# Mixer after pooled attention, one core: alpha1 spread by a DMA, the first batch's order of work changed

## The chip, the cores and the metric

The kernel runs on one core of one Trainium2 chip. The metric is the device time of one execution in microseconds; before the change it is 352.65 us, the median of three runs (352.64, 352.65 and 353.04). The profile is that of one further execution and covers a span of 351.1 us.

## The reference

Two blocks follow each other, for 8 batches of 576 tokens. Attention has 8 heads of 64; keys and values are averaged over groups of 8 tokens, so that each of the 576 queries meets 72 keys. Its output x, 576 x 512 for each batch, goes into a mixer:

```
k_p = k.reshape(B, H, Sp, 8, D).mean(axis=3)            # v_p alike
attn = softmax(q @ k_p.T / sqrt(D));  x = attn @ v_p
a1  = alpha1 * x + beta1
tok = einsum('ts,bsd->btd', w_tok, a1)
u   = x + lam * tok
ch  = relu((alpha2 * u + beta2) @ w_ch1) @ w_ch2
out = u + lam * ch
```

alpha1, beta1, alpha2, beta2 and lam are vectors over the 512 columns; w_tok is 576 x 576, w_ch1 512 x 2048, w_ch2 2048 x 512. Inputs and output are float32 in memory; matrices are multiplied in 16-bit types.

## The kernel before, in words

**Tiling.** A batch is cut into four chunks of 128 tokens and a rest of 64; two batches share one chunk for their rests. Nine blocks of four chunks go through the hidden layer. For a block, `mlp_A` (L604) makes one of 16 hidden slices of 128 x 512 and `mlp_B` (L638) turns all 16 into the output of one chunk.

**Order of work.** Each engine takes its instructions strictly in the order in which the program emits them, and waits where an operand or a buffer isn't ready. For blocks in the steady state the order comes from a list of due times that is sorted (at the end of the function). The attention and mix of batch 1 are worked into block 0 in this way, those of batch 2 into block 1, and so on. Batch 0 has nothing to be worked into: its order is written out by hand, call after call, ahead of the loop. Nearly all of the change is in this written order.

**Batch 0.** `att_F` transposes two heads' queries on TensorE and copies them to `qT`; heads 0 to 3 come from the first half of q, 4 to 7 from the second. `cast_rem` makes the 16-bit remainder rows (tokens 512 to 575) and `att_Frem` transposes its queries. `double_k` and `att_K` make the averaged keys; `first_V` the averaged values. `att_S` makes one head's scores (L455, L458) and exponentials on ScalarE (L460), `att_AV` its output (L519, L523), which VectorE divides by the row sum (L525, L527) into the tile `x`.

**The mix.** The operand of the token mix is `xs` = lam * alpha1 * x in 16 bits, made by `att_X` two heads at a time: L534 for the four full chunks, L538 for the rest of 64 rows. The product lam * alpha1, spread over 128 partitions, is `lamal_bc`. The term with beta1 is a row more of `xs` (`bias_row`, L258), which meets the row sums of w_tok. `setup_wtok(c)` transposes one column block of w_tok into `wtT` (copy on ScalarE, L299), and `setup_rowsum(c)` puts that block's row sums into a spare row of `wtT` (L308, L310). `mix_T(b, c)` multiplies one chunk (L567, five matmuls of 128 x 512; the fifth reads the rest rows of `xs`), adds x on VectorE to give u (L571), and multiplies by alpha2 into `u_bf` (L574, on VectorE or GpSimd). `mix_uT` transposes `u_bf` (L588) and copies it to `u_fm` (L590), the operand of `mlp_A`. `setup_bias` makes the hidden layer's bias from beta2 and w_ch1 (L349).

**How vectors are spread.** lam, alpha1 and beta1 come as rows into `vecs`. `broadcast` spreads a row by a matmul with a column of ones (L278) and copies it out of PSUM; for alpha1 VectorE multiplies by lam while it copies (L282). alpha2 is spread by a DMA instead (`load_al2`, L273), behind a memset of one column of its tile, so that the transfer can't start before a chosen point of VectorE's order.

**Queues.** SP and ScalarE issue some loads, GpSimd issues those that cast to 16 bits (q, w_tok, w_ch1, w_ch2, the first k and v). During the first 50 us GpSimd's queue always holds work. The later loads of SP are held by memsets on VectorE: al2, then the remainder rows of batch 1 (L119), then its k (L90).

**Buffers.** PSUM tiles named gp (`gp(...)`) take turns in six banks, two more serve the outputs of the hidden layer and the warm-up matmuls (`keep_warm`, L558: matmuls of 128 x 512 whose result nobody reads).

Of the kernel before, what the change touches and what calls it, by code (L numbers as in the profile page):

```python
# [7 lines left out]
FP = mybir.dt.float32  # L8
# [3 lines left out]
ALU = mybir.AluOpType  # L12
AX = mybir.AxisListType

P = 128
SPG = 72
DM = 512
# [6 lines left out]
def kernel(  # L24
# [18 lines left out]
    nc = tc.nc  # L43
    ctx.enter_context(tc.manual_schedule())
    B, H, S, D = q.shape
# [19 lines left out]
    st1 = {}  # L65
# [75 lines left out]
    def cast_rem(b, eng, copy=None):  # L141
        raw = st1[b]["rem_raw"]
        rq = work.tile([P, 2, 2, D], BF, tag="rem_q", bufs=2, name="rem_q")
        rk = work.tile([P, 2, 2 if b else 3, D], BF, tag="rem_k", bufs=2, name="rem_k")
        (copy or eng.tensor_copy)(out=rq.rearrange("p c h d -> p h c d"), in_=raw[:, 0])  # L145
        twice = [raw[:, 1, :, c].unsqueeze(2).to_broadcast((P, 2, 2, D)) for c in range(2)]
        if b:
            eng.tensor_tensor(out=rk, in0=twice[0], in1=twice[1], op=ALU.add)
        st1[b]["rem"] = rq, rk
# [27 lines left out]
    al2_bc = const.tile([P, DM], FP, tag="al2_bc", name="al2_bc")  # L177
    b2row = const.tile([4, P], FP, tag="b2row", name="b2row")

    vecs = const.tile([65, 4, DM], FP, tag="vecs", name="vecs")  # L180
    ones_row = const.tile([1, P], FP, tag="ones_row", name="ones_row")
    nc.vector.memset(ones_row, 1.0)

    def load_vector(i, src, queue=nc.scalar):
        n = 65 if i in (0, 3) else 1
        queue.dma_start(out=vecs[0:n:64, i],
                        in_=src.unsqueeze(0).to_broadcast((1 + n // 65, DM)))

    new_batch(0)
    load_vector(0, moe_lam)  # L190
    load_rem(0)
    load_q_bf(0, 0)
    load_k16(0, 0)
    load_vector(1, moe_alpha1, nc.sync)
    load_vector(3, moe_beta1, nc.sync)
    start = const.tile([1, 2], FP, tag="start", name="start")
    nc.vector.memset(start, 0.0)
    nc.scalar.activation(out=start[:, 1:2], in_=start[:, 0:1], func=AF.Exp, bias=0.0, scale=1.0)
# [56 lines left out]

    def bias_row(i):
        p0 = 64 - 64 * i
        nc.vector.tensor_tensor(out=xs_pool[i][p0:p0 + 1, 4, :], in0=vecs[p0:p0 + 1, 3],  # L258
                                in1=vecs[p0:p0 + 1, 0], op=ALU.mult)

    b2c_bf = const.tile([P, 4], BF, tag="b2c_bf", name="b2c_bf")
# [3 lines left out]
    def more_constants():  # L265
        nc.vector.memset(ones_bf, 1.0)
        nc.vector.memset(ones_lo[0:64], 1.0)
        nc.vector.memset(ones_lo[64:128], 0.0)
        nc.vector.memset(wtT[:, :, S:640], 0.0)

    def load_al2(behind):
        behind.memset(al2_bc[:, 0:1], 0.0)
        nc.sync.dma_start(out=al2_bc, in_=moe_alpha2.unsqueeze(0).to_broadcast((P, DM)))  # L273

    def broadcast(i, out, by=None):

        ps = gp("ps_bc")
        nc.tensor.matmul(out=ps, lhsT=ones_row, rhs=vecs[0:1, i])  # L278
        if by is None:
            nc.scalar.copy(out=out, in_=ps)  # L280
        else:
            nc.vector.tensor_tensor(out=out, in0=by, in1=ps, op=ALU.mult)  # L282

    def setup_vectors():
        ps = gp("ps_vec")
# [68 lines left out]
    def att_F(b, hp, copy=nc.scalar.copy):  # L354


        st = st1[b]
        u, r = hp // 2, hp % 2
        if r == 0:
            st["qT"][u] = work.tile([P, 8, P], BF, tag="qT", bufs=4, name="qT")  # L360
        if b > 1:
            if r == 0:
                nc.sync.dma_start_transpose(out=st["qT"][u],
                                            in_=st["q"][u].rearrange("p h c d -> p (h c d)"))
            return
        ps_q = gp("ps_q").bitcast(BF)
        for c in range(4):
            nc.tensor.transpose(
                out=ps_q[:, 128 * c:128 * c + 128],
                in_=st["q"][u][:, 2 * r + c // 2, 2 * (c % 2):2 * (c % 2) + 2].rearrange(  # L370
                    "p c d -> p (c d)"),
                identity=identity_bf)
        copy(out=st["qT"][u][:, 4 * r:4 * r + 4, :],
                       in_=ps_q[:, 0:512].rearrange("p (c t) -> p c t", c=4))
# [16 lines left out]
    def double_k(u):  # L391

        nc.vector.tensor_copy(out=st1[0]["k"][u][:, :, 4], in_=st1[0]["k"][u][:, :, 0])
        if u == 0:
            cast_rem_k(nc.vector)
# [52 lines left out]
    def att_S(b, h):  # L448
        st = st1[b]
        u, r, hh = h // 4, h // 2 % 2, h % 2  # L450
        ET = ET_pool[u][:, h % 4]
        for half in range(2):
            n0, n = 256 * half, 256 + 64 * half
            ps_sc = gp("ps_sc")
            nc.tensor.matmul(out=ps_sc[0:SPG, 0:256], lhsT=kpT_pool[u][:, half, h % 4, :],  # L455
                             rhs=st["qT"][u][:, 2 * (h % 4):2 * (h % 4) + 2, :])
            if half:
                nc.tensor.matmul(out=ps_sc[0:SPG, 256:320], lhsT=kpT_pool[u][:, hh, h % 4, :],  # L458
                                 rhs=st["rem_qT"][:, :, h // 2::4].rearrange("p c i -> p i c"))
            nc.scalar.activation(out=ET[:, n0:n0 + n], in_=ps_sc[0:SPG, 0:n],  # L460
                                 func=AF.Exp, bias=0.0, scale=0.125)
        st["ET"][h] = ET
# [45 lines left out]
    def att_AV(b, h):  # L508
        st = st1[b]
        if "x" not in st:  # L510
            st["x"] = st1[b - 1]["x"] if b % 2 else work.tile([P, 6, DM], FP, tag="x_tm", bufs=1, name="x_tm")
        hp, hh = h // 2, h % 2
        ET, vp1, x = st["ET"][h], vp1_pool[hp], st["x"]
        ps_av = gp("ps_av")
        av = ps_av[:, 0:5 * 66].rearrange("p (c x) -> p c x", x=66)
        odd = b % 2
        for c in range(4):
            m0 = 256 * (c % 2) + 128 * (c // 2)
            nc.tensor.matmul(out=av[:, odd + c, :], lhsT=ET[:, m0:m0 + 128],  # L519
                             rhs=vp1[:, hh, :])  # L520

        r0 = 512 - 64 * odd
        nc.tensor.matmul(out=av[:, 4 - 4 * odd, :], lhsT=ET[:, r0:r0 + 128], rhs=vp1[:, hh, :])  # L523
        rec = work.tile([P, 5], FP, tag="rec", bufs=2, name="rec")
        nc.vector.reciprocal(out=rec, in_=av[:, :, 64:65])  # L525
        dd = D * h
        nc.vector.tensor_tensor(out=x[:, 1 - odd:6 - odd, dd:dd + D], in0=av[:, :, 0:64],  # L527
                                in1=rec.unsqueeze(2).to_broadcast((P, 5, D)), op=ALU.mult)

    def att_X(b, h0, h1, eng=nc.vector):  # L530

        x, xs = st1[b]["x"], xs_pool[b % 2]
        cols = slice(D * h0, D * h1)
        eng.tensor_tensor(  # L534
            out=xs[:, 0:4, cols], in0=x[:, 1:5, cols],
            in1=lamal_bc[:, cols].unsqueeze(1).to_broadcast((P, 4, D * (h1 - h0))), op=ALU.mult)
        p0 = 64 * (b % 2)
        eng.tensor_tensor(out=xs[p0:p0 + 64, 4, cols], in0=x[p0:p0 + 64, 5 - 5 * (b % 2), cols],  # L538
                          in1=lamal_bc[p0:p0 + 64, cols], op=ALU.mult)


    st2 = {}
# [11 lines left out]
    def keep_warm(count):  # L554

        ps = psB.tile([P, DM], FP, tag="ch", bufs=2, name="ps_warm")
        for _ in range(count):
            nc.tensor.matmul(out=ps, lhsT=warm[:, 0:P], rhs=warm)  # L558
# [98 lines left out]
    load_q_bf(1, 0)  # L657
    load_q_bf(1, 1)
    load_w1(2)
    keep_warm(2)  # L660
    broadcast(0, lam_bc)
    keep_warm(2)
    att_F(0, 0)
    att_F(0, 1)
    more_constants()
    cast_rem(0, nc.vector)
    att_Frem(0, nc.scalar.copy)
    keep_warm(1)
    double_k(0)
# [5 lines left out]
    first_V(0, 0)  # L675
    att_S(0, 2)
    double_k(1)
    att_AV(0, 0)
    att_S(0, 3)
    keep_warm(1)  # L680
    att_K(0, 1, None)
    att_AV(0, 1)
    broadcast(1, lamal_bc, lam_bc)
    att_F(0, 2)
    att_F(0, 3, nc.vector.tensor_copy)
    att_X(0, 0, 2, nc.gpsimd)
    att_AV(0, 2)
    keep_warm(1)
    att_S(0, 4)
    first_V(0, 1)  # L690
    att_AV(0, 3)
    att_X(0, 2, 4, nc.gpsimd)
    load_al2(nc.vector)
    att_S(0, 5)
    setup_vectors()
    keep_warm(1)
    att_AV(0, 4)
    att_S(0, 6)
    keep_warm(1)
    att_AV(0, 5)  # L700
    load_rem(1, behind=nc.vector)
    att_X(0, 4, 6, nc.gpsimd)
    att_S(0, 7)
    setup_wtok(0, nc.scalar.copy)
    att_AV(0, 6)
    setup_wtok(1, nc.scalar.copy)
    att_AV(0, 7)
    for u in range(2):
        load_k(1, u, nc.vector)
    setup_rowsum(0)  # L710
    setup_wtok(2, nc.scalar.copy)
    setup_rowsum(1)
    setup_wtok(3, nc.scalar.copy)
    att_X(0, 6, 8)
    setup_rowsum(2)
    keep_warm(1)
    load_w1(3)
    load_v16(1, (0, 1))
    setup_rowsum(3)
    mix_T(0, 0, nc.gpsimd)  # L720
    mix_T(0, 1, nc.gpsimd)
    load_v16(1, (2,))
    for g in range(3):
        load_w2(g)
    setup_bias(0)
    mix_T(0, 2)
    mix_uT((0, 0))
    mix_T(0, 3)
    setup_wtok(4, nc.scalar.copy)
    mix_uT((0, 1))  # L730
    setup_bias(1)
    mlp_A(0, 0, 0, 256)
    mix_uT((0, 2))
    mlp_A(0, 1, 0, 256)
    mlp_A(0, 2, 0, 256)
    mix_uT((0, 3))
    mlp_A(0, 3, 0, 256)
# [54 lines left out]
    for n in range(NBLK):  # L792
# [16 lines left out]
        b = n + 1  # L809
# [45 lines left out]
```

The softmax here doesn't subtract the row's maximum and nothing guards it: scores larger than these inputs give would overflow.

## Time and profile before

| | |
|---|---|
| time, median of 3 | 352.65 us |
| span of the profiled execution | 351.1 us |
| TensorE busy | 337.8 us, 96% |
| VectorE, ScalarE, GpSimd busy | 226.0, 150.6, 78.9 us |
| first mix matmul (L567) | 23.99 us from the span's start |
| first hidden-layer matmul (L604) | 30.51 us |
| second halves of the first four hidden slices | from 33.10 us |
| w_tok's 576 KB and 72 KB, from issue to landing | 9.4 and 9.3 us |

Times in the profile are counted from the span's start, which is shorter than the device time by the start and end of the execution. Where a line of a timeline or of the chain of waits begins with two numbers, these are start and length. A busy engine is not by itself a bound: what matters is which wait ends last at the point in question, and for the first 33 us that changes from engine to engine. DMA lines give a queue (q0 is GpSimd's, q1 SP's, q10 ScalarE's), packets, megabytes, and the time of the packets as a share of 16 engines.

### The profile page before, as it was taken

The numbers are of one execution on the slowest core, as the hardware profiler recorded it, in microseconds if no ns is written. First come the engines' busy times: TensorE is split into PE (matmuls) and PEld (weight loads), VectorE is DVE, ScalarE is ACT, GpSimd is POOL, SyncE is SP. The second block draws the span as 40 slices with busy tenths as digits, with TensorE's granted clock in tenths as the row PEclk, the third lists the DMA queues.
The fourth block names the chain that finished last, engine by engine and source line by source line (L and its number), as shares of the span: only waits on it lengthen the run. The fifth ranks groups of instructions, "written<-read, shape, count | busy, mean of one in ns | idle before, by whom it ended". The sixth has DMA issues, their size and how long they took to land.

```text
span 351.1 us, 5881 instructions
## 1 busy us (share of the span) xinstructions
PE 337.8 (96%) x2206; PEld 178.8 (51%) x2247; DVE 226.0 (64%) x476; ACT 150.6 (43%) x283; POOL 78.9 (22%) x93
## 2 busy tenths in 40 slices
PE   7989999999999999999999999999999999999995
PEld 2667654455544554455445544554455445545544
DVE  6564048788696769775967697948785883037511
ACT  4564972238502850087008800791069105703800
POOL 8578600072017000710071005300510000000000
PEclk9999999999999999999999999999999999999999
DMA  8999980898738942897189719991820032011012
GB/s 129 196 213 241 217 151 0 188 248 174 134 113 203 216 63 66 231 190 121 55 224 189 127 52 211 186 146 51 228 75 1 32 90 77 0 60 62 0 54 66
DMA packets 66045, 44.57 MB, mean 127 GB/s; under 512 B 32409, under 2 KB 57309, under 8 KB 66018
## 3 DMA queue, kind: packets, MB, share of 16 engines
q1 hardware_dynamic: 50486, 33.18, 39.4%
q0 software_dynamic: 15072, 10.76, 21.1%
q8 instruction: 17, 0.28, 0.3%
q10 hardware_dynamic: 460, 0.27, 0.3%
q14 instruction: 10, 0.08, 0.1%
HBM read 38.30 MB, written 9.44 MB: 136 GB/s over the span
## 4 chain that ended last, share of the span: by engine, by line
PE 85%; DVE 8%; ACT 3%; issue 2%; POOL 1%; POOLq 0%; DVEq 0%; ACTq 0%
PE ps_h L604 33%; PE ps_ch L638 30%; PE ps_tok L567 12%; DVE x_tm L527 2%; PE ps_s L475 2%; PE ps_av L519 2%; DVE xs L534 2%; DVE v_u L443 1%; PE ps_ch L627 1%; ACT wtT L299 1%; PE ps_kp L405 1%; DVE rec L525 1%; PE ps_sc L455 1%; DVE ps_ch L644 1%; PE ps_v L431 1%
## 5 line engine op out<-in xcount | busy, mean ns | idle before, releaser
L609 ACT ACTIVATE Hj<-ps_h,bias_cols 128x512 bf16<-128x512 f32 x144 | 98.4, 689 | 150.7 <-PE ps_h L604 149.2
L604 PE MATMUL ps_h<-u_fm,w 128*128 128x512 bf16 (+1 forms) x571 | 132.2, 374 | 2.0 <-ACT Hj L609 0.5
L638 PE MATMUL ps_ch<-w,Hj 128*128 128x512 bf16 x543 | 128.7, 379 | 1.1 <-issue 0.6
L604 PEld LDWEIGHTS <-w 128*128 128x128 bf16 x592 | 63.9, 114 | 52.4 <-issue 4.0
L638 PEld LDWEIGHTS <-Hj 128*128 128x128 bf16 x560 | 52.8, 98 | 60.9 <-issue 1.6
L567 PE MATMUL ps_tok<-xs,wtT 128*128 128x512 bf16 (+3 forms) x200 | 44.8, 380 | 1.9 <-DVE xs L534 1.8
L644 DVE TENSOR_TENSOR ps_ch<-lam_bc,ps_ch 128x512 f32<-128x512 f32 x32 | 22.2, 693 | 33.2 <-PE ps_ch L638 33.0
L145 POOL CAST rem_q<-rem_raw 128x256 bf16<-128x256 f32 x7 | 3.3, 475 | 151.6 <-DMA rem_raw<-in_q_dram 151.6
L571 DVE TENSOR_TENSOR u_sb<-x_tm,ps_tok 128x512 f32<-128x512 f32 (+1 forms) x40 | 27.3, 683 | 11.3 <-PE ps_tok L567 11.2
L527 DVE TENSOR_TENSOR x_tm<-ps_av,rec 128x320 f32<-128x320 f32 x64 | 31.5, 492 | 2.3
L645 DVE TENSOR_TENSOR u_sb<-u_sb,ps_ch 128x512 f32<-128x512 f32 x35 | 24.0, 687 | 13.7 <-PE ps_ch L638 12.5
L504 ACT ACTIVATE ET<-ps_s 72x512 f16<-72x512 f32 x56 | 32.3, 591 | 0.0
L525 DVE RECIPROCAL rec<-ps_av 128x5 f32<-128x5 f32 x64 | 12.2, 190 | 30.2 <-PE ps_av L523 30.0
L567 PEld LDWEIGHTS <-wtT 128*128 128x128 bf16 (+3 forms) x200 | 16.9, 100 | 23.6 <-DVE xs L534 3.4
L443 DVE TENSOR_TENSOR v_u<-v_u 72x512 f32<-72x512 f32 (+1 forms) x48 | 27.3, 570 | 0.8
L574 DVE TENSOR_TENSOR u_bf<-u_sb,al_bc 128x512 bf16<-128x512 f32 x34 | 25.8, 758 | 2.5 <-DMA u_fm<-u_bf 1.4
L160 POOL TENSOR_TENSOR k_raw<-k_raw 128x512 f32<-128x512 f32 x14 | 19.1, 1367 | 13.1 <-DMA k_raw<-in_k_dram 12.6
L534 DVE TENSOR_TENSOR xs<-x_tm,lamal_bc 128x512 bf16<-128x512 f32 x29 | 20.1, 692 | 1.0
L519 PEld LDWEIGHTS <-ET 72*128 72x128 f16 x256 | 14.1, 97 | 8.9 <-issue 0.4
L162 POOL TENSOR_TENSOR k_bf<-k_raw 128x512 bf16<-128x512 f32 x14 | 17.8, 1275 | 1.1
L519 PE MATMUL ps_av<-vp,ET 72*128 72x66 f16 x256 | 15.8, 193 | 0.2 <-issue 0.2
L417 DVE CAST kp<-ps_kp 128x288 bf16<-128x288 f32 x14 | 6.4, 456 | 12.9 <-PE ps_kp L411 12.3
(119 smaller groups left out, 228.0 us busy)
## 6 DMA issues: line engine op xcount, KB each, us to landing
out_dram<-u_sb SPq DMA_DIRECT2D x32, 256.0 KB
k_raw<-in_k_dram SPq DMA_DIRECT2D x14, 512.0 KB
v_u<-in_v_dram SPq DMA_DIRECT2D x12, 512.0 KB
q_bf<-in_q_dram POOLq DMA_DIRECT2D x16, 256.0 KB, 6.6
w<-in_moe_w_ch_dram POOLq DMA_DIRECT2D x8, 512.0 KB, 14.6
v<-in_v_dram POOLq DMA_DIRECT2D x4, 256.0 KB, 9.8
rem_raw<-in_q_dram SPq DMA_DIRECT2D x15, 64.0 KB
rem_raw<-in_k_dram SPq DMA_DIRECT2D x15, 64.0 KB
```

Source lines behind the costliest of these rows:

```text
L443: nc.vector.tensor_tensor(out=t[:, :, 0:n], in0=t[:, :, 0:n], in1=t[:, :, n:2 * n], op=ALU.add)
L504: nc.scalar.activation(out=o, in_=i, func=AF.Exp, bias=0.0, scale=0.125)
L519: nc.tensor.matmul(out=av[:, odd + c, :], lhsT=ET[:, m0:m0 + 128], rhs=vp1[:, hh, :])
L527: nc.vector.tensor_tensor(out=x[:, 1 - odd:6 - odd, dd:dd + D], in0=av[:, :, 0:64], in1=rec.unsqueeze(2).to_broadcast((P, 5, D)), op=ALU.mult)
L534: eng.tensor_tensor(out=xs[:, 0:4, cols], in0=x[:, 1:5, cols], in1=lamal_bc[:, cols].unsqueeze(1).to_broadcast((P, 4, D * (h1 - h0))), op= ...
L567: nc.tensor.matmul(out=ps_tok[p0:p1], lhsT=wtT[0:kk, at, P * c:P * c + p1 - p0], rhs=xs_pool[i][0:kk, sc, :], start=(sc == 0), stop=(sc == 4))
L571: nc.vector.tensor_tensor(out=s["u"][p0:p1, :], in0=x[p0:p1, 1 + c if c < 4 else 5 - 5 * i, :], in1=ps_tok[p0:p1, 0:DM], op=ALU.add)
L574: eng.tensor_tensor(out=s["u_bf"], in0=s["u"], in1=al2_bc, op=ALU.mult)
L604: nc.tensor.matmul(out=ps_h[:, t0:t1], lhsT=w1_of(cc, j), rhs=u_fm[n][:, cc, t0:t1], start=(cc == 0), stop=(cc == 3))
L609: nc.scalar.activation(out=t, in_=ps_h, func=AF.Relu, bias=bias_cols[:, j:j + 1], scale=1.0)
L638: nc.tensor.matmul(out=ps, lhsT=Hj[n, j][:, 128 * m:128 * m + 128], rhs=w2[j // 4][:, j % 4, :], start=(j == 0), stop=(j == NJ - 1))
L644: nc.vector.tensor_tensor(out=ps, in0=lam_bc, in1=ps, op=ALU.mult)
```

## The change

It re-orders the first batch. alpha1 is no longer spread by a matmul but loaded into all 128 partitions by a DMA of 256 KB on SP's queue, behind a memset on VectorE, and multiplied by lam on VectorE after both copies of the second half of q. This takes two fp32 matmuls out of TensorE's order, ahead of the transposes of that half. The rest rows of `xs` are made for all 512 columns in one instruction on VectorE (`rest_X`) instead of two heads at a time, mostly on GpSimd. Scores of the later heads stand one place earlier in TensorE's order, w_tok's first two blocks ahead of the outputs of head 6, and the first mixes ahead of the row sums that they don't need. The first bias sums go ahead of the mix; GpSimd makes `u_bf` for chunks 0 and 2 instead of 0 and 1; the transposes of `u_bf` are dealt out differently. `cast_rem` goes ahead of some memsets, and a few warm-up matmuls are added and moved. `vecs` loses the rows that are no longer used.

```diff
-    load_vector(1, moe_alpha1, nc.sync)
-    load_vector(3, moe_beta1, nc.sync)
+    load_vector(1, moe_beta1, nc.sync)
...
+    def load_al1(behind):
+        behind.memset(lamal_bc[:, 0:1], 0.0)
+        nc.sync.dma_start(out=lamal_bc, in_=moe_alpha1.unsqueeze(0).to_broadcast((P, DM)))
...
+    def rest_X(b, h0, h1, eng=nc.vector):
+        x, xs = st1[b]["x"], xs_pool[b % 2]
+        cols, p0 = slice(D * h0, D * h1), 64 * (b % 2)
+        eng.tensor_tensor(out=xs[p0:p0 + 64, 4, cols], in0=x[p0:p0 + 64, 5 - 5 * (b % 2), cols],
+                          in1=lamal_bc[p0:p0 + 64, cols], op=ALU.mult)
...
-    keep_warm(2)
+    keep_warm(3)
     broadcast(0, lam_bc)
-    keep_warm(2)
+    keep_warm(3)
     att_F(0, 0)
     att_F(0, 1)
+    cast_rem(0, nc.vector)
     more_constants()
-    cast_rem(0, nc.vector)
+    keep_warm(1)
     att_Frem(0, nc.scalar.copy)
...
     double_k(1)
+    load_al1(nc.vector)
     att_AV(0, 0)
...
     att_AV(0, 1)
-    broadcast(1, lamal_bc, lam_bc)
     att_F(0, 2)
     att_F(0, 3, nc.vector.tensor_copy)
-    att_X(0, 0, 2, nc.gpsimd)
+    nc.vector.tensor_tensor(out=lamal_bc, in0=lamal_bc, in1=lam_bc, op=ALU.mult)
+    att_X(0, 0, 2, nc.gpsimd, False)
+    keep_warm(2)
+    att_S(0, 4)
     att_AV(0, 2)
     keep_warm(1)
-    att_S(0, 4)
+    att_S(0, 5)
     first_V(0, 1)
     att_AV(0, 3)
-    att_X(0, 2, 4, nc.gpsimd)
+    att_X(0, 2, 4, nc.gpsimd, False)
     load_al2(nc.vector)
-    att_S(0, 5)
+    att_S(0, 6)
     setup_vectors()
+    att_AV(0, 4)
     keep_warm(1)
-    att_AV(0, 4)
-    att_S(0, 6)
-    keep_warm(1)
+    att_S(0, 7)
     att_AV(0, 5)
     load_rem(1, behind=nc.vector)
-    att_X(0, 4, 6, nc.gpsimd)
-    att_S(0, 7)
+    att_X(0, 4, 6, nc.gpsimd, False)
     setup_wtok(0, nc.scalar.copy)
+    setup_wtok(1, nc.scalar.copy)
     att_AV(0, 6)
-    setup_wtok(1, nc.scalar.copy)
+    setup_rowsum(0)
     att_AV(0, 7)
     for u in range(2):
         load_k(1, u, nc.vector)
-    setup_rowsum(0)
     setup_wtok(2, nc.scalar.copy)
     setup_rowsum(1)
+    setup_bias(0)
     setup_wtok(3, nc.scalar.copy)
-    att_X(0, 6, 8)
-    setup_rowsum(2)
-    keep_warm(1)
+    att_X(0, 6, 8, nc.vector, False)
+    rest_X(0, 0, H)
     load_w1(3)
     load_v16(1, (0, 1))
+    mix_T(0, 0, nc.gpsimd)
+    setup_rowsum(2)
+    mix_T(0, 1)
     setup_rowsum(3)
-    mix_T(0, 0, nc.gpsimd)
-    mix_T(0, 1, nc.gpsimd)
     load_v16(1, (2,))
-    for g in range(3):
+    load_w2(0)
+    mix_T(0, 2, nc.gpsimd)
+    for g in range(1, 3):
         load_w2(g)
-    setup_bias(0)
-    mix_T(0, 2)
     mix_uT((0, 0))
     mix_T(0, 3)
+    mix_uT((0, 1))
     setup_wtok(4, nc.scalar.copy)
-    mix_uT((0, 1))
     setup_bias(1)
     mlp_A(0, 0, 0, 256)
+    mlp_A(0, 1, 0, 256)
     mix_uT((0, 2))
-    mlp_A(0, 1, 0, 256)
     mlp_A(0, 2, 0, 256)
     mix_uT((0, 3))
     mlp_A(0, 3, 0, 256)
```

More of the change, by code (lines that the diff above doesn't have):

```diff
@@ L178 @@
     b2row = const.tile([4, P], FP, tag="b2row", name="b2row")
-    vecs = const.tile([65, 4, DM], FP, tag="vecs", name="vecs")
+    vecs = const.tile([65, 2, DM], FP, tag="vecs", name="vecs")
     ones_row = const.tile([1, P], FP, tag="ones_row", name="ones_row")
@@ L184, in load_vector @@
     def load_vector(i, src, queue=nc.scalar):
-        n = 65 if i in (0, 3) else 1
-        queue.dma_start(out=vecs[0:n:64, i],
-                        in_=src.unsqueeze(0).to_broadcast((1 + n // 65, DM)))
+        queue.dma_start(out=vecs[0:65:64, i], in_=src.unsqueeze(0).to_broadcast((2, DM)))
     new_batch(0)
@@ L257, in bias_row @@
         p0 = 64 - 64 * i
-        nc.vector.tensor_tensor(out=xs_pool[i][p0:p0 + 1, 4, :], in0=vecs[p0:p0 + 1, 3],
+        nc.vector.tensor_tensor(out=xs_pool[i][p0:p0 + 1, 4, :], in0=vecs[p0:p0 + 1, 1],
                                 in1=vecs[p0:p0 + 1, 0], op=ALU.mult)
@@ L273, in load_al2, with broadcast @@
         nc.sync.dma_start(out=al2_bc, in_=moe_alpha2.unsqueeze(0).to_broadcast((P, DM)))
-    def broadcast(i, out, by=None):
+    def broadcast(i, out):
         ps = gp("ps_bc")
         nc.tensor.matmul(out=ps, lhsT=ones_row, rhs=vecs[0:1, i])
[L279 to L282, printed above, removed]
+        nc.scalar.copy(out=out, in_=ps)
     def setup_vectors():
@@ L528, in att_AV, with att_X @@
                                 in1=rec.unsqueeze(2).to_broadcast((P, 5, D)), op=ALU.mult)
-    def att_X(b, h0, h1, eng=nc.vector):
+    def rest_X(b, h0, h1, eng=nc.vector):
[3 more added lines that the diff above has]
+                          in1=lamal_bc[p0:p0 + 64, cols], op=ALU.mult)
+    def att_X(b, h0, h1, eng=nc.vector, rest=True):
         x, xs = st1[b]["x"], xs_pool[b % 2]
@@ L536, in att_X @@
             in1=lamal_bc[:, cols].unsqueeze(1).to_broadcast((P, 4, D * (h1 - h0))), op=ALU.mult)
-        p0 = 64 * (b % 2)
-        eng.tensor_tensor(out=xs[p0:p0 + 64, 4, cols], in0=x[p0:p0 + 64, 5 - 5 * (b % 2), cols],
-                          in1=lamal_bc[p0:p0 + 64, cols], op=ALU.mult)
+        if rest:
+            rest_X(b, h0, h1, eng)
     st2 = {}
```

## The prediction

> **What bounds the kernel now.** I read the page first (busy shares, slices), then the chain of waits for the first 33 us, then the instruction timelines of each engine there, then the DMA view in narrow windows. The page's first part says that the whole is TensorE's:
>
> ```profile
> PE 337.8 (96%) x2206; PEld 178.8 (51%) x2247; DVE 226.0 (64%) x476; ACT 150.6 (43%) x283; POOL 78.9 (22%) x93
> ```
>
> From about 33 us on the chain is nearly all matmul, so whatever delays or advances the first hidden-layer matmuls (L604, second halves, at 33.10) moves the end by the same amount. All edits lie ahead of that. The chain of waits there (start, length, what; all in us):
>
> ```profile
> 19.12 1.37 ACT ET L460 x4
> 20.50 1.18 ACT wtT L299 x2
> 21.69 0.26 ACT wtT L310
> 21.97 0.70 ACT wtT L299
> 22.69 0.26 ACT wtT L310
> 22.97 0.70 ACT wtT L299
> 23.71 0.44 PE ps_rs L308 x5
> 24.15 2.17 PE ps_tok L567 x10
> 26.32 0.50 PE ps_bias L349 x16
> 32.46 0.60 ACT u_fm L590
> 33.06 0.04 issue
> ```
>
> To be seen: the first mix (L567) starts at 24.15 because ScalarE hands out the w_tok copies and row sums one after another until 23.7. VectorE is hardly better (start, length, line):
>
> ```profile
> 15.94 0.68 DVE L282 TENSOR_TENSOR lamal_bc<-lam_bc,ps_bc 128x512 f32<-128x512 f32 x1
> 16.53 0.42 DVE L373 COPY qT<-ps_q 128x512 bf16<-128x512 bf16 x1
> 17.82 0.48 DVE L436 CAST vp<-ps_v 72x128 f16<-72x128 f32 x2 [0.25 <-PE ps_v L433]
> 21.79 0.69 DVE L534 TENSOR_TENSOR xs<-x_tm,lamal_bc 128x512 bf16<-128x512 f32 x1
> 22.41 0.54 DVE L538 TENSOR_TENSOR xs<-x_tm,lamal_bc 64x128 bf16<-64x128 f32 x1
> ```
>
> From lam*alpha1 at 15.94 to the last rows of xs at 22.95 it is busy all but about a quarter of a microsecond. So the mix has two near-equal predecessors, ScalarE's (23.95) and VectorE's (22.95). The edit shortens the first and puts a DMA wait at the head of the second. The model for that DMA is the al2 load, of the same size and queue:
>
> ```profile
> 18.99 0.37 SPq L273 DMA_DIRECT2D al_bc<-in_moe_alpha_dram  x1
> ```
>
> The DMA view from 18.9 to 22.6, then from 22.6 to 24.6 (packets, MB, share):
>
> ```profile
> q0 software_dynamic: 961, 0.74, 129.5%
> ```
> ```profile
> q0 software_dynamic: 436, 0.22, 83.1%
> q1 hardware_dynamic: 148, 0.26, 39.2%
> ```
>
> For 3.6 us after its issue not one packet of the SP queue (q1) moves; GpSimd's queue (q0) has all engines. Then 0.26 MB go in some 1.5 us. The load's last landing event in the trace is at 24.52: **5.5 us from issue to landing**.
>
> [...] a 128x512 warm-up matmul takes 0.43 us at 8.09, four hidden-layer 128x512 take 0.86 at 36.5, and the granted clock is recorded from about 12.0 on. [...]
>
> **The change, part by part.**
>
> *Start.* Two more warm-up matmuls before 6.2 fill a DMA wait (0.46 at 2.88), and one fills the 0.63 that TensorE waited at 7.69 for the cast of the remainder, which now precedes the four memsets of 0.7 in all. Counting: warm-ups to 6.24, eight transposes 1.03, warm-up 0.43, two transposes 0.39, warm-up 0.43 = 8.52, where L405 began in the chain at 8.51. The k sums need the remainder's k anyway (cast at 7.90). So nothing moves unless the clock rises earlier: zero here, a rival below.
>
> *Alpha1.* Removed: the K=1 matmul pair L278, 1.05 on TensorE at 14.50, with the transposes of the second q half behind it. These go at 14.5 instead of 15.55. Added: a memset after the k copy on VectorE (13.11 + 0.23, so 13.40), the SP issue at 13.45, 256 KB. Landing L = 13.45 + latency. Low: 2.7 to the first packet, about what SP transfers at 81.0 and 112.1 show, with a q load of GpSimd's queue ahead of them (2.6 and 2.8), plus 1.9 = 4.6, L = 18.05. Middle: al2's 5.5, L = 18.95. High: behind w_tok and all of w1's first group, whose landing events end at 20.55, L = 20.4. I take 5.0, **L = 18.45**, because w_tok's large packets end at about 16 and al1 may then have its turn.
>
> *VectorE.* Program order puts the product lam*alpha1 right after the copy of qT. Unstalled it would start at 16.3 (the copy of 0.33 after AV1's 15.95). So VectorE stands still for some 2 us, until L. Behind it in its queue: AV2's two instructions, the casts of v, AV3 to AV7. From the rows: product 0.62; AV2 0.66; casts 0.42; AV3 to AV7 5 x 0.66 = 3.3; memsets 0.15: X(6,8) starts at L + 5.2 and ends at L + 5.9 (before, from 16.57 to 21.79 is the same work). Removed from the end: the 0.54 rest rows; added one 64x512 product, 0.69, ending at L + 6.5. The mix needs it only for its fifth matmul, 0.87 after its start: hidden. GpSimd loses three rest operations (0.44, 0.45, 0.90): off the path.
>
> *TensorE and ScalarE meanwhile.* The PSUM ring "gp" has six banks: the second half of S6 takes AV2's bank, free at L + 1.3, that of S7 AV3's, at L + 2.4. So both wait for VectorE too. Then exp of S7 to L + 3.05, w_tok copies 0.6 + 0.6, row sum 0.26: row sum 0 done at L + 4.6, under VectorE's L + 5.9. Mix 0 no longer stands behind w_tok's third copy, row sums 2 and 3 (about 1.2 of ScalarE's chain); this is what the reordering earns, and the alpha wait takes it back. **Mix 0 starts at L + 5.9 = 24.35**, against 24.15.
>
> *From mix 0 to the second halves.* Before 33.10 - 24.15 = 8.95. Of it 0.5 is w_tok's last copy ahead of u_fm on ScalarE (29.54 to 30.46) and 0.66 the last u_fm copy. After, from M = start of mix 0: mix 0, row sum 2, mix 1, row sum 3, mix 2 = 3 x 1.08 + 2 x 0.2 = 3.64; uT 0.23 (u_bf of GpSimd ready: 1.12 + 0.69 + 1.3 = 3.15, in time); mix 3 1.08; uT 0.23 = 5.18; the copy of u_fm goes ahead of w_tok's and ends at 5.8; TensorE has w_tok's fifth block 0.3 and the bias sums 0.5 until 5.98; A 0, A 1, uT, A 2, uT, A 3 = 4 x 0.44 + 2 x 0.23 = 2.2, to 8.2; wait for the last u_fm copy to **M + 8.4**. A gain of 0.55. Moving the first bias sums ahead and swapping which u_bf GpSimd makes are in these sums.
>
> *Sum.* 24.35 + 8.4 = 32.75, against 33.10: -0.35. Against it 0.1 for what VectorE's wait sets off on SP: al2's memset at L + 2.4 = 20.9 (18.88 before), the remainder's at 22.2 (20.35), so the second batch's k moves about 1.8 later on a queue that showed
>
> ```profile
> 33.62 1.27 POOL L160 TENSOR_TENSOR k_raw<-k_raw 128x512 f32<-128x512 f32 x1 [1.20 <-DMA k_raw<-in_k_dram]
> ```
>
> k_raw lands at L + 17.0 = 35.45, its two sums take 2.6, k_bf is ready at 38.1, where TensorE wants it at 38.47 - 0.35 = 38.1: a tie. al2 itself, at 20.9 + 5.5 = 26.4, is wanted at M + 1.87 = 26.2 with 0.5 to spare. Forecast 352.65 - 0.35 + 0.1, rounded: **352.4 us**, in effect no change.
>
> **Rivals.** *Earlier start, faster.* [...] K, S and V of the first heads shrink by some 0.8 (20 small matmuls 0.96 to 0.7, S 1.0 to 0.55, then the second k half's landing limits), and the memset comes at 12.5. Or alpha1 needs only 4 us. Either takes 0.8 to 1.2: 351.3. For: the three idle stretches are filled. Against: [...] L may be set by w_tok's packets whatever the issue. *Late alpha1, slower.* L = 20.4: M = 26.3, second halves at 34.7, +1.6: 354.2. For: al2 waited for 961 packets, 60 per engine, which from 13.45 would reach into w1. Against: those two SP transfers waited for about 400. *Second batch late, slower.* The tie at 38.1 goes wrong by about 1: 353.5. For: the 1.20 wait above. Against: alpha1's time shifts both sides of the tie alike.
>
> **How the numbers follow.** Forecast 0.40, earlier start 0.34, late alpha1 0.18, late second batch 0.08. 0.2% is 0.7 us: faster is the second case and a little of the first, 0.38; slower the last two less a little, 0.24; same 0.38. The range takes the ends 351.0 (both halves of the faster rival) and 354.2 (late alpha1).
>
> **What would show it.** VectorE idle before the lam*alpha1 product, ended by a DMA on lamal, from about 16.3 to 18.5; the first L567 at L + 5.9 with xs as its releaser, not ScalarE; 8.4 from there to the second halves; no wait for k_bf at L405 near 38. A 128x512 warm-up or S matmul at half its length before 12 shows the clock rival. Wrong would be: alpha1 landing before 17.5 or after 19.5, or a new PSUM wait on TensorE longer than VectorE's.

## The result, and the profile after

The changed kernel is slower: 356.11 us, median of 4 runs (355.6 to 357.01), against 352.64 us for the kernel before beside it (4 runs, 352.59 to 353.04). The ratio is 1.0099, 95% interval 1.0075 to 1.0122, or about 3.5 us. The profiled execution has a span of 353.5 us, the shortest of the four (the others 353.7 to 354.9); before it was 351.1. So the profile shows 2.4 us of the loss.

The page of the changed kernel, its first part and the clock row of its second:

```profile
PE 338.4 (96%) x2207; PEld 179.9 (51%) x2248; DVE 225.3 (64%) x477; ACT 150.8 (43%) x283; POOL 77.3 (22%) x90
...
PEclk9969999999999999999999999999999999999999
```

To be seen: the busy times have hardly moved, but one digit of the clock row is a 6. It is the third slice, 17.7 to 26.5 us. Before, all forty are 9. In the records of the granted clock behind that row TensorE is at full clock from 8.44 to 18.68, **at half clock from 18.68 to 25.50**, then full until the work ends.

The second halves of the hidden slices, where the prediction put its mark, before and after:

```profile
33.10 1.91 PE L604 MATMUL ps_h<-u_fm,w 128*128 128x256 bf16 x16 [0.24 <-ACT u_fm L590]
```
```profile
35.18 1.91 PE L608 MATMUL ps_h<-u_fm,w 128*128 128x256 bf16 x16 [0.24 <-ACT u_fm L594]
```

They are 2.08 us late, so nearly all of the profile's 2.4 is lost ahead of this point. Where, is told by the timelines of VectorE and TensorE (start, length, line; in brackets the idle time ahead of it and what ended it):

```profile
12.39 0.06 DVE L269 MEMSET lamal_bc<- 128x1 f32 x1
...
14.98 0.42 DVE L371 COPY qT<-ps_q 128x512 bf16<-128x512 bf16 x1
19.16 0.69 DVE L691 TENSOR_TENSOR lamal_bc<-lamal_bc,lam_bc 128x512 f32<-128x512 f32 x1 [3.76 <-DMA lamal_bc<-in_moe_alpha_dram]
...
20.39 0.47 DVE L434 CAST vp<-ps_v 72x128 f16<-72x128 f32 x2
...
23.74 0.20 DVE L523 RECIPROCAL rec<-ps_av 128x5 f32<-128x5 f32 x1 [0.61 <-PE ps_av L521]
```
```profile
17.03 0.22 PE L284 MATMUL ps_vec<-identity,b2row 4*128 4x4 f32 x1
20.72 0.38 PE L517 MATMUL ps_av<-vp,ET 72*128 72x66 f16 x4 [3.47 <-DVE vp L434]
...
22.17 1.26 PE L294 MATMUL ps_w<-identity_bf,wt_bf 128*128 128x128 bf16 x10
...
26.32 1.25 PE L571 MATMUL ps_tok<-xs,wtT 128*128 128x512 bf16 x4
```

VectorE reaches the lam*alpha1 product 3.76 us before alpha1 is there and stands still. Behind the product in its queue is the cast of the averaged values of heads 4 to 7; their last matmul (L431) ends at 16.54, and the cast runs at 20.39, after the product. TensorE's next attention output (head 4) needs that cast, so TensorE stands still for 3.47 us too, from 17.25 to 20.72, and its clock falls to half 1.4 us into this wait. When work comes back it runs slowly: ten transposes of w_tok take 1.26 us; in the first experiment, at full clock, the same ten take 0.73. VectorE, which divides these outputs before it can make `xs`, now waits for TensorE in its turn: 0.26, 0.61 and 0.22 us ahead of heads 5 to 7. In the kernel with TensorE kept at full clock (below) these three waits are gone.

The chain of waits of the changed kernel, part of 8 to 36 us, to be set beside the one in the prediction:

```profile
12.49 6.64 DMA lamal_bc<-in_moe_alpha_dram
19.13 0.02 issue
19.16 0.69 DVE lamal_bc L691
...
20.72 0.38 PE ps_av L517 x4
...
22.36 1.07 PE ps_w L294 x10
...
23.70 0.67 PE ps_rs L306 x5
...
26.48 0.22 PE ps_tok L571
```

Before, ScalarE's copies of w_tok led up to the mix. Now it is alpha1's DMA, 6.64 us from issue to landing, and after it TensorE at half clock. Where the load loses its time is seen in the DMA view, 12.5 to 15.9 and then 15.9 to 19.2:

```profile
q0 software_dynamic: 479, 0.72, 117.6%
```
```profile
q0 software_dynamic: 391, 0.42, 76.7%
q1 hardware_dynamic: 144, 0.26, 25.5%
```

For about 3.5 us after the issue nothing of SP's queue moves. Then its 0.26 MB take 3.1 us (first packet 15.97, last landing event 19.13), beside GpSimd's queue. Of that queue's 391 packets in the second window 299 are of 1 KB. w_tok's large packets, of 4.6 KB, had nearly all moved before: 117 of 128 in the first window, 11 in the second.

### The profile page after: what moved, and what is told of

Read it like the earlier page. It is cut to its first block, busy times and chain, and to the rows that moved or that the text cites. A ratio compares the mean times of both kernels' runs of the same rounds, so it can differ in the third digit from the quotient of the medians.

```text
span 353.5 us, 5877 instructions
## 1 busy us (share of the span) xinstructions
PE 338.4 (96%) x2207; PEld 179.9 (51%) x2248; DVE 225.3 (64%) x477; ACT 150.8 (43%) x283; POOL 77.3 (22%) x90
## 4 chain that ended last, share of the span: by engine, by line
PE 85%; DVE 7%; DMA 4%; issue 2%; POOL 1%; ACT 1%; POOLq 0%; DVEq 0%; ACTq 0%
PE ps_h L608 34%; PE ps_ch L642 30%; PE ps_tok L571 12%; DVE x_tm L525 2%; PE ps_av L517 2%; PE ps_s L473 2%; DMA lamal_bc<-in_moe_alpha_dram 2%; DVE xs L539 2%; DMA k<-in_k_dram 2%; PE ps_ch L631 1%; DVE rec L523 1%; PE ps_bias L347 1%; PE ps_w L294 1%; PE ps_r L480 1%; PE ps_rs L306 1%
## 5 line engine op out<-in xcount | busy, mean ns | idle before, releaser
L571 PE MATMUL ps_tok<-xs,wtT 128*128 128x512 bf16 (+2 forms) x199 | 44.9, 381 | 2.0 <-DVE xs L539 1.8
L649 DVE TENSOR_TENSOR u_sb<-u_sb,ps_ch 128x512 f32<-128x512 f32 x35 | 24.1, 687 | 13.7 <-PE ps_ch L642 12.5
L571 PEld LDWEIGHTS <-wtT 128*128 128x128 bf16 (+3 forms) x200 | 16.9, 100 | 23.3 <-DVE xs L539 3.4
L441 DVE TENSOR_TENSOR v_u<-v_u 72x512 f32<-72x512 f32 (+1 forms) x48 | 28.1, 586 | 0.8
```

The costliest lines, as they stand in the source:

```text
L441: nc.vector.tensor_tensor(out=t[:, :, 0:n], in0=t[:, :, 0:n], in1=t[:, :, n:2 * n], op=ALU.add)
L571: nc.tensor.matmul(out=ps_tok[p0:p1], lhsT=wtT[0:kk, at, P * c:P * c + p1 - p0], rhs=xs_pool[i][0:kk, sc, :], start=(sc == 0), stop=(sc == 4))
L649: nc.vector.tensor_tensor(out=u, in0=u, in1=ps, op=ALU.add)
```

## The experiments

Theory A: VectorE's wait for alpha1 is the loss, with TensorE idle behind it and its clock falling. Rival B: the new order of work is itself worse. Rival C: the 256 KB on the queues are the loss, by delaying other loads. Ratios are to the kernel before on the same chip, with 95% intervals; each profile is of one execution. 0.1% is 0.35 us. The kernel before had medians of 352.64 us beside the changed kernel and of 353.21 to 353.59 beside the others, so a difference of two rows is less sure than either ratio, and the profiles' marks are given next to it. "Kept warm" stands for TensorE kept at full clock by matmuls that nobody reads. Lines of the same instruction differ by a few numbers from kernel to kernel.

| kernel | ratio | half clock, us | first mix | second halves |
|---|---|---|---|---|
| before | 1 | none after 12.0 | 23.99 | 33.10 |
| changed | 1.0099 [1.0075, 1.0122] | 18.68 to 25.50 | 26.32 | 35.18 |
| changed, alpha1 by matmul | 0.9931 [0.9907, 0.9955] | none after 9.8 | 22.58 | 31.46 |
| before, alpha1 by DMA | 1.0115 [1.0078, 1.0152] | 21.02 to 24.43 | 27.89 | 37.01 |
| changed, TensorE kept warm | 1.0032 [1.0017, 1.0048] | none after 10.3 | 25.23 | 34.17 |
| changed, load at the start | 0.9982 [0.9965, 1.0] | 11.89 to 18.72 | 25.17 | 34.03 |
| changed, load issued 1.7 us earlier | 1.004 [1.0021, 1.006] | 19.60 to 26.43 | 26.09 | 35.13 |
| changed, load on GpSimd's queue | 0.9988 [0.9964, 1.0011] | 21.13 to 27.96 | 24.96 | 35.30 |
| changed, product later | 1.0046 [1.0017, 1.0075] | 25.05 to 28.46 | 24.50 | 35.04 |
| the same, kept warm | 1.0005 [0.9989, 1.002] | none after 10.3 | 24.32 | 33.17 |
| alpha1 by matmul, idle load beside it | 0.9949 [0.9928, 0.9971] | none after 9.0 | 22.35 | 31.23 |
| before, new start only | 0.9989 [0.9972, 1.0005] | none after 10.1 | 23.28 | 32.39 |
| alpha1 by matmul, old start | 0.9953 [0.9931, 0.9975] | none after 11.2 | 22.99 | 31.87 |
| alpha1 by matmul, old tail | 0.9978 [0.9965, 0.9991] | none after 7.8 | 22.72 | 31.83 |

**alpha1 by matmul again.** Everything else of the change stays; the matmul stands behind the transposes of q's second half, not ahead of them.

```diff
-    load_al1(nc.vector)
...
-    nc.vector.tensor_tensor(out=lamal_bc, in0=lamal_bc, in1=lam_bc, op=ALU.mult)
+    broadcast(2, lamal_bc, lam_bc)
```

> The changed kernel with alpha1 spread by the old matmul pair (after both transposes of the second q half), all other edits kept. Theory A (the wait of VectorE for alpha1's DMA is the loss): no wait of several us at the product, TensorE doesn't idle from 17 to 21, the second halves of the first hidden slices begin near 30 instead of 35.2, and the time is about 350.2 us (349 to 351.5), under both kernels. Rival B (the new order is itself worse): at or above 352.6. Rival C (the 256 KB more on the DMA queues delay what comes later): some gain against 356.1, but no more than 1 us.

351.31 us, 0.9931: faster than both kernels. The product is at 15.74, VectorE waits for no DMA, the clock stays full. These are the lines of its TensorE timeline that answer to the ones above:

```profile
19.22 0.73 PE L298 MATMUL ps_w<-identity_bf,wt_bf 128*128 128x128 bf16 x10
...
22.58 1.25 PE L575 MATMUL ps_tok<-xs,wtT 128*128 128x512 bf16 x4 [0.17 <-DVE xs L543]
...
31.46 1.91 PE L612 MATMUL ps_h<-u_fm,w 128*128 128x256 bf16 x16 [0.24 <-ACT u_fm L598]
```

So rival B falls. By the ratios the new order, its start included, gains 2.4 us, and the DMA costs about 5.9 (0.9931 to 1.0099); at the second halves of the profiles, which had been expected near 30, it is a gain of 1.6 and a cost of 3.7.

**The DMA alone, in the old order**, issued at the same place, behind the second averaged keys' copies.

```diff
     double_k(1)
+    load_al1(nc.vector)
...
-    broadcast(1, lamal_bc, lam_bc)
+    nc.vector.tensor_tensor(out=lamal_bc, in0=lamal_bc, in1=lam_bc, op=ALU.mult)
```

> The kernel before with alpha1 spread by the DMA alone: memset after the second k copy on VectorE, the product where the old one stood, nothing else moved. Theory A: VectorE waits from about 16 to 19 or later, and TensorE falls idle for 3 us or more behind it; time 356 to 357.5 us. Rival B: near 352.6. The copy of the second half's qT stands behind the product here, so the loss may be larger than in the changed kernel.

357.74 us, 1.0115, with the same wait on VectorE and 4.1 us of TensorE behind it, here for the copy of `qT`. The DMA alone is about as bad as the whole change:

```profile
19.65 0.69 DVE L687 TENSOR_TENSOR lamal_bc<-lamal_bc,lam_bc 128x512 f32<-128x512 f32 x1 [4.16 <-DMA lamal_bc<-in_moe_alpha_dram]
```

**TensorE kept warm in the wait.** 15 matmuls that nobody reads, ahead of head 4's output.

```diff
+    keep_warm(15)
     att_AV(0, 4)
```

> The changed kernel with 15 warm-up matmuls (3.2 us at full clock) on TensorE ahead of head 4's output, where it idles for 3.5 us. The wait for alpha1 stays. If the fall of the clock from 18.7 to 25.5 is a loss of its own, the rate there stays full and the time falls by about 1.3 us, to 354.8; the runs should also lie closer together. If VectorE's queue alone sets the start of the mix (alpha1's landing plus 5.9, as the prediction had it), nothing changes: 356.

354.25 us, 1.0032. VectorE waits as before, but the clock stays full (14 of the 15 are in the trace):

```profile
19.39 0.69 DVE L691 TENSOR_TENSOR lamal_bc<-lamal_bc,lam_bc 128x512 f32<-128x512 f32 x1 [3.83 <-DMA lamal_bc<-in_moe_alpha_dram]
```
```profile
17.38 3.19 PE L562 MATMUL ps_warm<-warm 128*128 128x512 bf16 x14 [0.16 <-issue]
...
25.23 1.24 PE L571 MATMUL ps_tok<-xs,wtT 128*128 128x512 bf16 x4 [0.25 <-DVE xs L539]
```

The load landed at 19.36, and the mix starts 5.87 us after that, against 7.19 in the changed kernel. This splits the loss. From 1.0099 to 1.0032 is the half clock: 0.67% or 2.4 us by the ratios, 1.9 by the plain medians, 1.3 at the mix, counted from the landing, in the two profiles. From 1.0032 to 0.9931 is the wait itself: 1.0% or 3.6 us by the ratios, 2.9 by the medians, 2.7 at the second halves. The product ends 3.66 us later here than with the matmul (20.08 against 16.42).

**The load at the start**, without the memset, behind beta1's, issued at 3.07.

```diff
     load_vector(1, moe_beta1, nc.sync)
+    nc.sync.dma_start(out=lamal_bc, in_=moe_alpha1.unsqueeze(0).to_broadcast((P, DM)))
...
-    load_al1(nc.vector)
```

> The changed kernel with alpha1's DMA issued at the start on SP's queue, held by nothing. Theory A: alpha1 is there by 9, VectorE doesn't wait for it, and the time is under that of the kernel before, about 351 us; the loads behind it (remainder, second k half, second q half) come up to 1.3 us later (256 KB at 200 GB/s), so it stays some 0.5 to 1 above the matmul version. Rival C (256 KB more are the loss): about as slow as the changed kernel.

353.04 us, 0.9982: the wait is gone (landed at 9.57), but not all of the loss. The 256 KB now stand beside the first loads, and v comes at 11.9 to 12.3 instead of 9.5 to 9.9:

```profile
11.97 1.07 PE L430 MATMUL ps_v<-v,pool_v 128*72 128x256 f16 x4 [0.95 <-DMA v<-in_v_dram]
```

In this wait the clock fell to half, at 11.89. The bytes do cost something here, where every load is awaited.

**The load issued earlier**, its memset right after the first averaged keys.

```diff
     att_K(0, 0, None)
+    load_al1(nc.vector)
...
-    load_al1(nc.vector)
```

> The changed kernel with alpha1's memset, and so its DMA, directly behind the first averaged keys on VectorE (near 10.1 instead of 12.4); the product stays where it is. If alpha1's landing sets the start of the mix (landing plus 5.9 while the clock stays up), the landing at 15.7 to 16.9 leaves at most 1.5 us of wait, the clock doesn't fall, the mix starts at 22 to 23, ratio 0.993 to 0.997. If the loss came from the 256 KB in the queues or from the rest of the order: no better than 1.003.

354.92 us, 1.004. The issue moved from 12.49 to 10.81, the landing only from 19.13 to 18.66: the first packet came at 14.48 instead of 15.97, and the transfer took 4.2 us instead of 3.1. VectorE's wait shrinks to 2.73 and TensorE's to 2.64, and the clock falls all the same. By its number this run is on the rival's side of the expectation, but what theory A was to be tried on, a landing at 15.7 to 16.9, did not come about.

The runs of this kernel price the clock without a second kernel. One stretch of 3.41 us at half clock makes a mean clock of 0.995. The 11 runs at 0.993 to 0.995 have a median of 354.35 us, the six at about 0.99 (two stretches) 355.61, the three at about 0.985 (three stretches) 356.96: some 1.3 us for each stretch, if what brought the stretches cost nothing besides.

**The load on GpSimd's queue, ahead of w_tok.**

```diff
+    nc.gpsimd.dma_start(out=lamal_bc, in_=moe_alpha1.unsqueeze(0).to_broadcast((P, DM)))
     load_wtok()
...
-    load_al1(nc.vector)
```

> The changed kernel with alpha1's 256 KB put on GpSimd's own queue, ahead of w_tok, instead of on the sync engine's queue behind VectorE's memset. Theory A (what costs is VectorE standing still until alpha1 has landed, and TensorE idle with it): in its own place in the queue the spread lands at 15.5 to 16.5 us instead of 19.13, before VectorE wants it; no long wait on VectorE's lamal product, the clock stays full, and the ratio is 0.993 to 0.996, as with the spread by matmuls. w_tok lands some 1.3 us later (256 KB at about 200 KB/us) and its transposes may wait for it by up to 1 us, which would give part of this back. Rival C (the 256 KB themselves cost what is lost): 1.000 or above.

352.6 us, 0.9988, short of what theory A had here. alpha1 landed at 16.66 and VectorE waits 0.89 us only. But w_tok lands at 20.55 and 20.87 instead of 18.01 and 19.36, more than the 1.3 us that I had allowed, and TensorE waits for it:

```profile
20.60 0.83 PE L295 MATMUL ps_w<-identity_bf,wt_bf 128*128 128x128 bf16 x10 [1.37 <-DMA wt_bf<-in_moe_w_tok_dram]
```

The clock fell at 21.13 for 6.83 us. This profiled execution was the longest of the 14 timed (356.37); others, at a mean clock of 0.997 or more, took 351.1 to 353.6. One wait was exchanged for another.

**The same bytes, awaited by nobody.** alpha1 by matmul, and the changed kernel's load besides, into a spare buffer (`load_spare` is `load_al1` with another target).

```diff
     double_k(1)
+    load_spare(nc.vector)
```

> The fastest kernel so far (the changed kernel with alpha1 spread by matmuls), and besides it the changed kernel's load of alpha1, at the same place of the sync engine's queue behind the same memset, into a spare buffer that nothing reads. Theory A (the wait costs, not the bytes): 0.993 to 0.9955, as without this load; at most some tenths of a microsecond for w_tok and w1 that land later. Rival C (the 256 KB on the queues cost a good part of the 3.5 us): 0.998 or above, with w_tok's transposes or the bias sums waiting for a DMA.

351.58 us, 0.9949; without the load it was 0.9931, inside the interval. The load landed at 19.07, like the changed kernel's, and the second halves start at 31.23. So at this place in the queue the bytes cost 0.6 us by the ratios, which their intervals can't tell from nothing, and nothing in the profiles (31.46 without them). Rival C isn't the cause.

**The product later**, behind the output of head 5, so that VectorE has work until alpha1 lands; GpSimd makes `xs` for heads 0 to 3, VectorE for 4 to 7.

```diff
+    nc.vector.tensor_tensor(out=lamal_bc, in0=lamal_bc, in1=lam_bc, op=ALU.mult)
+    att_X(0, 0, 2, nc.gpsimd, False)
+    att_X(0, 2, 4, nc.gpsimd, False)
...
+    att_X(0, 4, 8, nc.vector, False)
```

> The changed kernel with the DMA issued as there, but the product lam * alpha1 after head 5's output on VectorE; GpSimd then makes xs for heads 0 to 3, VectorE for 4 to 7 in one. If the place of the waiting instruction in VectorE's queue is the loss, not the DMA: VectorE reaches the product near 19.4, when alpha1 has landed (19.1), TensorE never idles, its clock stays up, the mix starts near 23, and the time is within 0.3 us of the matmul version (ratio 0.993 to 0.995). If the DMA's traffic costs something of its own, it stays nearer to 1.000.

355.5 us, 1.0046. VectorE waits 0.27 us for the DMA, as meant, but the mix then waits for GpSimd:

```profile
20.90 3.55 POOL L539 TENSOR_TENSOR xs<-x_tm,lamal_bc 128x512 bf16<-128x512 f32 x2 [6.72 <-DVE lamal_bc L706]
...
23.25 1.75 DVE L532 TENSOR_TENSOR xs<-x_tm,lamal_bc 64x512 bf16<-64x512 f32 x1
...
24.50 1.79 PE L571 MATMUL ps_tok<-xs,wtT 128*128 128x512 bf16 x4 [1.69 <-POOL xs L539]
```

GpSimd's two products take 1.78 us each, against 1.27 in the changed kernel, and VectorE's rest rows 1.75 against 0.68: they work at the same time here. But VectorE's product of 128x1024 in the same stretch (22.11 to 23.34) took 1.23 us, less than two of 128x512 at 0.69, so what lengthens the others is not shown. The clock fell at 25.05. One of the ten runs, at a mean clock of 0.999, took 352.1 us.

**The same, kept warm.**

```diff
+    keep_warm(8)
     mix_T(0, 0, nc.gpsimd)
```

> The kernel with alpha1's product moved behind the fifth attention sum (the run with the product later), with 8 warm-up matmuls on TensorE ahead of the first mix. If what that kernel lost was the fall of TensorE's clock during the wait for the scaled rows: ratio about 0.997, no half clock before the second halves. If it was the wait itself, for the rows that GpSimd scales more slowly while VectorE scales too: 1.003 to 1.005, as without the warm-ups.

353.28 us, 1.0005, between the two numbers expected. The clock was 0.41% of the 1.0046, or 1.4 us. What stays against the fastest kernel, 0.74%, goes with a mix that starts 1.74 us later (24.32 against 22.58), behind GpSimd's rows, which can't start before the product at 19.93.

**The start edits alone**, and **the fastest kernel without them**:

```diff
-    keep_warm(2)
+    keep_warm(3)
...
+    cast_rem(0, nc.vector)
     more_constants()
-    cast_rem(0, nc.vector)
+    keep_warm(1)
```

> The kernel before with the start edits alone: three warm-up matmuls instead of two at both places, one more ahead of the remainder's transposes, and the remainder's cast ahead of the memsets. If the filled idle stretches let TensorE's clock double earlier (8 to 10.5 instead of 12 in the profile), the first heads come up to 0.8 us earlier and the time falls by 0.5 to 1 us (ratio 0.997 to 0.9985). If the earlier clock in the changed kernel was chance or hidden, ratio 1.000.

> The changed kernel with alpha1 spread by the matmul (as in the first experiment) and the old start. What is left is the new order from the second half of q to the hidden layer. If the gain of the first experiment (ratio 0.9931, second halves 1.64 us earlier) is the order's, ratio 0.994 to 0.996; if it is the start's, 0.999 to 1.001.

352.87 us, 0.9989 with them alone; 351.73 us, 0.9953 without them, against 0.9931 with. So they gain 0.4 to 0.8 us, neither clear of nothing by its interval. In the profiles the clock rises at 10.06 instead of 12.03, and at 9.75 instead of 11.24; the second halves come 0.71 and 0.41 earlier.

**The fastest kernel with the old order from w_tok's transposes on** (the rest rows stay in one go).

```diff
     setup_rowsum(1)
-    setup_bias(0)
...
+    setup_rowsum(2)
+    keep_warm(1)
...
-    mix_T(0, 0, nc.gpsimd)
-    setup_rowsum(2)
-    mix_T(0, 1)
     setup_rowsum(3)
+    mix_T(0, 0, nc.gpsimd)
+    mix_T(0, 1, nc.gpsimd)
...
```

> The fastest kernel so far (the changed kernel with alpha1 spread by matmuls) with the old order from w_tok's transposes on: the first mixes go back behind w_tok's last row sums; the last rows of the mix's operand stay in one go. If the gain of the new order comes from there: half or more of the 0.7% is given back, ratio about 0.9965 or above. If it comes from q's second half and the scores starting earlier: 0.993 to 0.995, as before this edit.

352.47 us, 0.9978. By the ratios two thirds of the order's 0.7% is given back (0.9931 to 0.9978); by the profiles less than a quarter, 0.37 of 1.64 us at the second halves. The tail gains something, but how much stays open: the two kernels were timed on different chips.

## Why the prediction was wrong, by its own steps

The marks of its sum, forecast and measured (us):

| term | forecast | measured | difference |
|---|---|---|---|
| alpha1 lands, L | 18.45 | 19.13 | +0.68 |
| L to the first mix | 5.9 | 7.19 | +1.29 |
| first mix to second halves | 8.4 | 8.86 | +0.46 |
| second halves | 32.75 | 35.18 | +2.43 |

**The step that failed** is "TensorE and ScalarE meanwhile". It saw that TensorE would wait behind VectorE, priced that only by when PSUM banks come free for the scores of heads 6 and 7 (those of head 6 ran at 16.64, before the wait), and let TensorE go on at full clock. It didn't follow the second thing behind the product in VectorE's queue, the cast of v, to the matmul that needs it; and it gave no thought to what 3.5 us of idleness do to the clock. Here a wait of 3.47 us went with 6.82 us at half clock, and the fall came 1.4 us into the wait. The kernel kept warm shows what that cost (1.3 us at the mix; 2.4 us by the ratios). With full clock the sum L + 5.9 is right: 5.87. Of the prediction's own signs of being wrong none came: alpha1 landed between 17.5 and 19.5, and no PSUM wait outlasted VectorE's. A falling clock was not among them.

**alpha1's landing** was mis-sized, and the earlier issue hid part of it. Memset and issue came a microsecond earlier than forecast (12.49, not 13.45), but the latency was 6.64, not 5.0. I took less than al2's 5.5 on the ground that alpha1 may begin to move when w_tok's large packets end. It did begin about then, at 15.97, 3.5 us after the issue. What was too small was the transfer: 3.1 us to the landing, beside 1 KB packets, not the 1.9 that I had. The high case, behind w_tok and w1 (L = 20.4), didn't come either. The late-alpha1 rival (354.2) had the sign, but with a landing later than it was and without the clock.

**From mix to second halves** a gain of 0.25 was seen, not 0.55. The prediction mixed two marks: its 24.15 is where the chain has the first mix, 0.16 later than its start in the timeline (23.99 before; 26.48 and 26.32 after). Counted from the start it was 9.11 before and is 8.86 here, 8.88 and 8.94 in the two kernels at full clock. A mix took 1.08 as forecast; the row sums between took 0.28 each, not 0.2, and the second bias sums 0.62, not 0.5 (the chain). With the 0.16 between the marks and a little waiting this is the +0.46.

**What held.** VectorE stood still where forecast, with the releaser forecast, though for 3.76 us and not some 2: it got there earlier, and alpha1 later. The 64x512 rest rows took 0.68, as priced by estimate (0.69, what the trace has for 128x512); the mix waits for `xs` and not for ScalarE when the clock is full; no wait for `k_bf` near 40.7, so the late-second-batch rival didn't happen. The start at zero was perhaps a little low: the earlier-start rival's clock is seen (a rise at 10.06 instead of 12.03 with the start edits alone), for some 0.4 to 0.8 us that are not clear of nothing; that filled stretches would bring the rise forward was an estimate of the prediction. And "this is what the reordering earns, and the alpha wait takes it back" has the right signs and the wrong sizes: by the ratios the order with alpha1 by matmul earns 2.4 us, the wait takes 3.6, the clock 2.4 more.

In the profile 2.43 of the miss is explained term by term. The medians of the runs differ by 1.1 us more than the two profiles do; all four runs of the changed kernel had a mean clock of 0.988 to 0.99, so none escaped the half clock, but what the longer ones lost besides isn't shown.

## What to carry to other kernels

The load that replaced an on-chip spread of some 1.1 us (before, L278) took 6.64 us from issue to landing, 3.5 of them without a packet of its own while another queue moved 0.74 MB: price such a load with what the other queues are moving when it is issued. Its wait, 3.76 us here, held up everything behind the waiting instruction in VectorE's order: follow each of those to the engine that needs it. If that engine is TensorE, add up its work: in these profiles half clock came after steps of 3.41 us with 3028 columns or fewer, less than two fifths of the 8100 that full-clock matmuls fill by estimate (last section). Price that (0.67% here, by the ratios), or keep TensorE warm. And look at a change of many parts by undoing the one with the new wait: here that turned +1.0% into -0.7%.

## What the runs showed of the hardware that was not expected

**An earlier issue brought an earlier first packet, and hardly an earlier landing.** With GpSimd's queue at work, the first packet of a load on SP's came 3.5 to 3.7 us after the issue, and in between that queue moved 0.73 MB for al2 before, 0.74 for alpha1 after, 0.71 for al2 after, 0.76 for alpha1 issued earlier, in 493 packets or in 1155. A store of SP's queue at 61.36, with GpSimd's queue idle, had its first packet after 0.87 us. Once a transfer had begun, both queues moved: while the 128 packets of 2 KB of the load moved, GpSimd's queue moved 255 to 269, about two for one, in all four, and the time to the last packet went with their size. It was 1.5 and 1.6 us for al2, beside packets mostly of 512 B, 2.6 for alpha1, beside 1 KB, and 3.7 for alpha1 issued earlier, with 67 of w_tok's 4.6 KB packets among them. So the earlier issue ended in a slower transfer. What the silence before waits for isn't shown: GpSimd's queue moved 199 to 214 GB/s in it (before and changed kernel), so a fixed amount can't be told from a fixed delay.

**The clock fell after short waits.** It fell with single waits of TensorE of 4.1, 3.47 and 2.64 us, and also where the longest was 1.69, 1.37 or 0.95 us (product later; load on GpSimd's queue; load at the start), in the profiles always for one or two times 3.41 us (3.41 or 6.83), and a whole number of times 3.41 us after the rise (10.24, three times, in the changed kernel). What sets them apart in these traces is the work in one step of 3.41 us, counted from the rise: the columns of the moving operands, 512 for a 128x512 matmul, of all matmuls that began in it. The steps just ahead of the six falls have 4 to 3028 columns (3022 in the changed kernel, from 15.27 to 18.68), those ahead of the falls at the end of the work 2048 at most. Every other step at full clock in the 14 profiles has 3328 or more; by estimate a full one would have some 8100, as four 128x512 matmuls take 0.86 us. Busy time tells less: a step with 2.09 us of small attention matmuls (load at the start, 8.48 to 11.89) went ahead of a fall, and two at the end of the work, with 1.61 us of 128x512 ones, did not. No run was made to try this count.

**VectorE's and GpSimd's products took longer side by side**: 1.78 us instead of 1.27 for those of `xs` on GpSimd (product later), and 1.75 instead of 0.68 for the 64x512 one on VectorE, the latter in both kernels with the product later. VectorE's 128x1024 there, at 1.23 us, is the exception that isn't explained.
